# Attention kernel, one core: VectorE and TensorE streams as loops, one exponential per block, stores begun by SyncE

## Chip, cores, metric

One Trainium2 chip, one core. The metric is device time in microseconds (us) of one execution, the median of several. The kernel before takes 640.71 us (three runs, 640.48 to 640.77).

## The reference

```python
B, H, Sq, Skv, Dh = 8, 16, 16, 2048, 256          # bfloat16
def reference(q, k, v):
    scale = q.shape[-1] ** -0.5
    scores = jnp.einsum('bhqd,bhkd->bhqk', q, k) * scale
    attn = softmax(scores, axis=-1)
    return jnp.einsum('bhqk,bhkd->bhqd', attn, v)
```

There are 128 heads with 16 queries each. K and V are 134 MB each and are read once, so the work is 269 MB of loads with little arithmetic on each byte.

## The kernel before

Eight heads make a block; there are 16 blocks (`g`), each with two halves (`e`) of four heads. A half needs one K load and one V load of 4.19 MB. In each block:

- VectorE transposes K (`kt`, four pieces per half), copies the probabilities into the layout that PV needs (`px`), takes the maximum of S, and transposes P (`pt`).
- TensorE does S = QK (64 matmuls), then PV of the block before (64 matmuls).
- ScalarE does the exponential, spreads the next block's queries into QW (`qwb`), and evacuates half of the output (`evac_a`), that is, scales it and copies it out of `O_ps`.
- SyncE issues all loads. ScalarE issues the stores.

A small scheduler writes each engine's stream as a list of jobs; a job waits for the semaphores of the jobs that it depends on. The parts that matter here:

```python
def emit_exp(eng, g, h):                      # one half of S at a time
    return eng.activation(P_sb[:, 1024 * h:1024 * h + 1024],
                          S_ps[:, 2 * h:2 * h + 2, :].rearrange("p c n -> p (c n)"), ACTF.Exp,
                          bias=negm[:, g:g + 1], scale=1.0, accum_out=lsum[:, g, h:h + 1])
# ... (cut)
for g in range(G):                            # SyncE: loads only
    for u in (2 * g, 2 * g + 1):
        k_load(u)                             # waits: the transposes that read this K buffer
    if g:
        for u in (2 * g - 2, 2 * g - 1):
            v_load(u)                         # waits: PV of the block that used this V buffer
# ... (cut)
for g in range(G):                            # ScalarE
    if g >= 2:
        evac_a(g - 2)
    qwb(g + 1, 0)
    if g >= 2:
        store(g - 2)                          # two output buffers, O_fin[:, g % 2, :]
    qwb(g + 1, 1)
    softmax_act(g)                            # two exponentials
# ... (cut)
for g in range(G):                            # VectorE, all 16 blocks written out
    for e in range(2):
        for c in range(4):
            if g != 1 or e or c > 1:
                kt(g, e, c)
    if g >= 2:
        evac_b(g - 2)
    if g:
        px(g - 1, 0)
        px(g - 1, 1)
    dve_max(g)
    # ... (cut)
    for h in range(2):
        dve_pt(g, h)
    small(g)                                  # 1 / sum, times the mask
# ... (cut): TensorE: block 0 written out, blocks 1 to 14 as a hardware loop, block 15 written out
```

## Time and profile before

| | before |
|---|---|
| time | 640.71 us |
| bytes moved, mean rate from 60 to 592 us | 270.65 MB, 431 GB/s |
| TensorE / VectorE / ScalarE busy | 77% / 67% / 16% |
| VectorE's idle ahead of the transposes of K | 159.7 us in all |

From the page of the kernel before: busy time (us, share of the span, instructions), the busy tenths of the DMA engines in 40 slices, and the DMA queues (packets, MB, share of 16 engines).

```profile
span 639.2 us, 4824 instructions
...
PE 489.1 (77%) x2176; PEld 166.7 (26%) x1680; DVE 427.8 (67%) x372; ACT 99.1 (16%) x208; POOL 4.2 (1%) x7
...
DMA  9999999999999999999999999999999999999996
...
q1 hardware_dynamic: 13488, 269.51, 98.7%
q10 hardware_dynamic: 2288, 1.03, 0.6%
q8 instruction: 4, 0.07, 0.0%
q14 instruction: 6, 0.05, 0.0%
```

The DMA engines are full from the first slice to the last but one. No compute engine comes near that. q1 is SyncE's queue (loads); q10 is ScalarE's (stores); q8 and q14 fetch instructions.

The chain of waits that ended last, four pieces of it from the steady state (start us, us, what):

```profile
242.54 30.13 DMA KN<-in_k_dram
272.69 8.90 DVE KB L126 x4
281.61 30.36 DMA KN<-in_k_dram
311.99 8.90 DVE KB L126 x4
```

This reads like a latency loop: a load, four transposes that free its buffer, the next load. It isn't one, because the 30 us are mostly time in the queue behind other loads, and the DMA engines never pause. One block in the VectorE timeline (start us, us, instruction, [idle before it, and what ended that]):

```profile
282.41 8.89 DVE L126 STREAM_TRANSPOSE KB<-KN 128x2048 f32<-128x2048 f32 x4 [0.83 <-DMA KN<-in_k_dram]
291.22 0.45 DVE L313 SCALAR_TENSOR_TENSOR O_fin<-O_ps,rab,O_tmp 128x256 bf16<-128x256 f32 x1
291.58 3.44 DVE L163 COPY PT<-PC 32x1024 bf16<-32x1024 bf16 x8
295.06 2.29 DVE L148 TENSOR_REDUCE negm<-S_ps 128x1 f32<-128x2048 f32 x1
298.67 2.37 DVE L157 STREAM_TRANSPOSE PC<-P_sb 128x1024 bf16<-128x1024 bf16 x2 [1.32 <-ACT P_sb L152]
...
301.31 0.23 DVE L292 TENSOR_SCALAR rab<-mask,rinv 128x2 f32<-128x2 f32 x1
311.99 8.89 DVE L126 STREAM_TRANSPOSE KB<-KN 128x2048 f32<-128x2048 f32 x4 [10.45 <-DMA KN<-in_k_dram]
```

Two numbers are 1.32 us (wait for the exponential) and 10.45 us (wait for K, VectorE's reserve in this block: the time that it could work more before anything else became late).

### The profile page before, as it was taken

Reading aid. Unit: us, or ns where it says so; the run is one execution under the profiler, and the core shown is the slowest. Engines: PE = TensorE matmul, PEld = TensorE weight load, DVE = VectorE, ACT = ScalarE, POOL = GpSimd, SP = SyncE. Lnnn points to the kernel's source line nnn. Section 1 sums busy time; section 2 is a strip of 40 time slices with the busy share of each in tenths; the row PEclk is TensorE's granted clock in tenths of the full one; section 3 lists DMA queues with packets and bytes.
Section 4 is the critical chain, followed back from the end, with each engine's and each line's share of the span. In section 5 each row is a group of like instructions: output and inputs, shape, how many; then the busy total and the mean of one; then the engine's idle time right before and its main releaser. Section 6 shows DMA issues by size and latency. Waiting matters only on the chain.

```text
span 639.2 us, 4824 instructions
## 1 busy us (share of the span) xinstructions
PE 489.1 (77%) x2176; PEld 166.7 (26%) x1680; DVE 427.8 (67%) x372; ACT 99.1 (16%) x208; POOL 4.2 (1%) x7
## 2 busy tenths in 40 slices
PE   0857879676896768868689686787967878676998
PEld 0111313123131221312214122131311313122287
DVE  4879386693857949387492965938669395693861
ACT  2121112030120301212011120211203012030010
POOL 2000000000000000000000000000000000000000
PEclk9979979799897999899898998997979989899899
DMA  9999999999999999999999999999999999999996
GB/s 322 428 431 426 432 433 441 435 427 428 421 438 429 431 429 429 437 439 425 437 414 443 431 429 431 425 430 433 437 441 425 432 417 440 429 429 430 421 427 258
DMA packets 15786, 270.65 MB, mean 423 GB/s; under 512 B 1824, under 2 KB 4128, under 8 KB 4640
## 3 DMA queue, kind: packets, MB, share of 16 engines
q1 hardware_dynamic: 13488, 269.51, 98.7%
q10 hardware_dynamic: 2288, 1.03, 0.6%
q8 instruction: 4, 0.07, 0.0%
q14 instruction: 6, 0.05, 0.0%
HBM read 269.48 MB, written 1.05 MB: 423 GB/s over the span
## 4 chain that ended last, share of the span: by engine, by line
DMA 67%; DVE 25%; PE 7%; issue 1%; SPq 0%; DVEq 0%
DMA KN<-in_k_dram 67%; DVE KB L126 23%; PE O_ps L177 4%; PE S_ps L143 1%; PE S_ps L131 1%; DVE negm L148 0%; DVE PC L157 0%; SPq L110 0%; DVE PT L163 0%; DVE O_fin L323 0%; DVE O_fin L313 0%; DVE rab L292 0%; DVE rinv L291 0%; DVEq L410 0%; DVE ltot L289 0%
## 5 line engine op out<-in xcount | busy, mean ns | idle before, releaser
L126 DVE STREAM_TRANSPOSE KB<-KN 128x2048 f32<-128x2048 f32 x128 | 284.6, 2281 | 159.7 <-DMA KN<-in_k_dram 139.3
L143 PE MATMUL S_ps<-KB,QW 128*128 128x512 bf16 x528 | 213.1, 413 | 125.2 <-DVE KB L126 125.2
L171 PE MATMUL O_ps<-VB,PT 128*128 128x512 bf16 x896 | 200.7, 386 | 22.2 <-DMA VB<-in_v_dram 22.2
L131 PE MATMUL S_ps<-KB,QW 128*128 128x512 bf16 x496 | 203.9, 411 | 0.0
L143 PEld LDWEIGHTS S_ps<-KB,QW 128*128 128x128 bf16 x528 | 54.0, 103 | 327.7 <-issue 239.4
L171 PEld LDWEIGHTS O_ps<-VB,PT 128*128 128x128 bf16 x896 | 87.9, 99 | 138.0 <-issue 38.6
L119 ACT ACTIVATE QW<-QT 32x128 bf16<-32x128 bf16 x128 | 53.9, 421 | 320.5 <-PE S_ps L131 312.8
L163 DVE COPY PT<-PC 32x1024 bf16<-32x1024 bf16 x128 | 53.3, 416 | 4.3 <-PE O_ps L177 2.6
L157 DVE STREAM_TRANSPOSE PC<-P_sb 128x1024 bf16<-128x1024 bf16 x32 | 37.9, 1223 | 19.8 <-ACT P_sb L152 19.8
L152 ACT ACTIVATE P_sb<-S_ps,negm 128x1024 bf16<-128x1024 f32 x32 | 35.4, 1110 | 36.3 <-DVE negm L148 26.7
L148 DVE TENSOR_REDUCE negm<-S_ps 128x1 f32<-128x2048 f32 x16 | 36.7, 2292 | 4.6 <-PE S_ps L131 4.1
L308 ACT ACTIVATE O_tmp<-O_ps,rab 128x256 f32<-128x256 f32 x15 | 7.1, 474 | 157.9 <-PE O_ps L171 157.1
L177 PE MATMUL O_ps<-KN,PT 128*128 128x256 bf16 x128 | 14.4, 273 | 0.0
L177 PE MATMUL O_ps<-VB,PT 128*128 128x256 bf16 x128 | 14.1, 273 | 0.1
L177 PEld LDWEIGHTS O_ps<-VB,PT 128*128 128x128 bf16 x128 | 12.4, 98 | 2.0 <-DVE PT L163 0.6
L177 PEld LDWEIGHTS O_ps<-KN,PT 128*128 128x128 bf16 x128 | 12.4, 98 | 1.8 <-DMA KN<-in_v_dram 0.3
L323 DVE TENSOR_SCALAR O_fin<-O_ps,rab 128x256 bf16<-128x256 f32 x2 | 1.0, 483 | 11.5 <-PE O_ps L177 11.5
L313 DVE SCALAR_TENSOR_TENSOR O_fin<-O_ps,rab,O_tmp 128x256 bf16<-128x256 f32 x15 | 6.7, 448 | 1.8 <-issue 1.8
L152 ACT ACTIVATION_READ_ACCUMULATOR P_sb<-S_ps,negm 128x1 f32 x32 | 6.3, 196 | 0.0
L113 DVE STREAM_TRANSPOSE QT<-VB 128x2048 f32<-128x2048 f32 x1 | 2.3, 2311 | 5.5 <-DMA VB<-in_q_dram 5.5
L292 DVE TENSOR_SCALAR rab<-mask,rinv 128x2 f32<-128x2 f32 x16 | 3.7, 228 | 0.6
L190 POOL MEMSET PT<- 128x4096 f32 x1 | 3.5, 3512 | 0.0
(11 smaller groups left out, 7.8 us busy)
## 6 DMA issues: line engine op xcount, KB each, us to landing
KN<-in_k_dram SPq DMA_DIRECT2D x28, 4096.0 KB, 30.1
VB<-in_v_dram SPq DMA_DIRECT2D x32, 2048.0 KB, 26.5
VB<-in_v_dram SPq DMA_DIRECT2D x14, 4096.0 KB, 20.0
KN<-in_k_dram SPq DMA_DIRECT2D x8, 2048.0 KB, 15.3
KN<-in_v_dram SPq DMA_DIRECT2D x2, 2048.0 KB, 27.6
KN<-in_v_dram SPq DMA_DIRECT2D x2, 1024.0 KB, 23.1
KN<-in_v_dram SPq DMA_DIRECT2D x3, 512.0 KB, 25.8
VB<-in_q_dram SPq DMA_DIRECT2D x4, 256.0 KB, 4.4
```

The source lines that it names most:

```text
L119: ins = eng.activation(ap_of(dv, dv.offset + 32 * a + e, [[256, 4], [128, 2], [2, 16]]), ap_of(sv, sv.offset + 2 * (2 * g + e), [[64, 4], ...
L126: return eng.transpose(KBf[:, c % R_KB].rearrange("p t i -> p (t i)"), KNf[:, e].rearrange("p t i -> p (t i)")[:, n * c:n * c + n])
L131: return eng.add_instruction(mybir.InstMatmult(start_tensor_calc=start, stop_tensor_calc=stop, ldweights=False, tile_size=(128, 128), tile ...
L143: ins = mm(S_ps[:, 2 * h + c, :], QW[:, e, bp, :], rhs, start=(e == 0 and bp == 0), stop=(e == 1 and bp == 7))
L148: return eng.tensor_reduce(out=negm[:, g:g + 1], in_=S_ps[:].rearrange("p c n -> p (c n)"), axis=AX.X, op=ALU.max, negate=True)
L152: return eng.activation(P_sb[:, 1024 * h:1024 * h + 1024], S_ps[:, 2 * h:2 * h + 2, :].rearrange("p c n -> p (c n)"), ACTF.Exp, bias=negm[ ...
L157: return eng.transpose(PC[:, h].rearrange("p t x -> p (t x)"), P_sb[:, 1024 * h:1024 * h + 1024])
L163: ins = eng.tensor_copy(PT[pr, 32 * h:32 * h + 32, pr], PC[pr, h])
L171: ins = eng.matmul(O_ps[:, 0, :], PT[:, t, :], rhs, start=(t == 0), stop=(t == NT - 1))
L177: ins = eng.matmul(O_ps[:, bank, 0:D], PT[:, t, :], buf[:, t, :], start=(t == 0), stop=(t == NT - 1))
L308: j_ea[g] = J("act", "ea", lambda eng: eng.activation(O_tmp[:], src, ACTF.Copy, scale=rab[:, g, 0:1]), [("pv", g, 1) if g < last - 1 else ...
L313: j_eb[g] = J("dve", "eb", lambda eng: eng.scalar_tensor_tensor(out=O_fin[:, g % 2, :], in0=src, scalar=rab[:, g, 1:2], in1=O_tmp[:], op0= ...
```

## The change

Its intent is a shorter program with fewer operations and waits: VectorE's blocks 2 to 15 become a loop; TensorE's loop takes in block 0 and branches around PV in its first turn; each block has one exponential over 2048 columns instead of two over 1024, and so no sum of two partial sums; stores 0 to 12 go to SyncE's queue, right behind the two K loads of a later block; one output buffer serves all but the last block; and waits that follow from earlier ones are left out. The scale `rab` of a block is copied to a second place, since the loop can't index it by block.

```diff
-        def emit_exp(eng, g, h):
-            return eng.activation(P_sb[:, 1024 * h:1024 * h + 1024], ...
+        def emit_exp(eng):
+            return eng.activation(P_sb[:], S_ps[:].rearrange("p c n -> p (c n)"), ACTF.Exp,
+                                  bias=negm[:], scale=1.0, accum_out=lsum[:])
 # ... (cut) SyncE
             for u in (2 * g, 2 * g + 1):
                 k_load(u)
+            if g >= 3:
+                store("sp", g - 3)
 # ... (cut) ScalarE
             if g >= 2:
                 evac_a(g - 2)
-            qwb(g + 1, 0)
-            if g >= 2:
-                store(g - 2)
-            qwb(g + 1, 1)
+            if g == last:
+                store("act", g - 2)
             softmax_act(g)
+            qwb(g + 1)
 # ... (cut) VectorE
             if g:
+                old_rab(g - 1)
                 px(g - 1, 0)
 # ... (cut) one output buffer: block g's evacuation waits for the store of block g-1
-                op0=ALU.mult, op1=ALU.add), [("pv", g, 1), ("ea", g), ("st", g - 2) if g >= 2 else None], inc=STEP)
+                op0=ALU.mult, op1=ALU.add), [("pv", g, 1), ("ea", g), ("st", g - 1) if g else None])
 # ... (cut) the loops
+        turns = {"dve": [order["dve"][dve_head + n * x:dve_head + n * x + n] for x in range(G - 2)],
+                 "pe": [order["pe"][0:4]] + [order["pe"][6 * x - 2:6 * x + 4] for x in range(1, last)]}
+            with nc.Fori(0, STEP * len(ts), STEP, engines=engines, head_slot={eng.engine: slot}) as it:
```

More of the change, by code (lines that the diff above doesn't have):

```diff
@@ L14 @@
 R_KB = 4
+PE_SLOT, DVE_SLOT = 8, 80
 STEP = 16
@@ L58, in bass_standalone__softmax_full_bidir__sampling_kernel @@
         O_tmp = ec(nc.sbuf_tensor("O_tmp", [128, D], F32))
-        O_fin = ec(nc.sbuf_tensor("O_fin", [128, 4, D], BF16))
+        O_fin = ec(nc.sbuf_tensor("O_fin", [128, 3, D], BF16))
         ident = ec(nc.sbuf_tensor("ident", [128, 128], BF16))
         mask = ec(nc.sbuf_tensor("mask", [128, 2], F32))
-        negm = ec(nc.sbuf_tensor("negm", [128, G], F32))
-        lsum = ec(nc.sbuf_tensor("lsum", [128, G, 2], F32))
-        ltot = ec(nc.sbuf_tensor("ltot", [128, G], F32))
-        rinv = ec(nc.sbuf_tensor("rinv", [128, G], F32))
-        rab = ec(nc.sbuf_tensor("rab", [128, G, 2], F32))
+        negm = ec(nc.sbuf_tensor("negm", [128, 1], F32))
+        lsum = ec(nc.sbuf_tensor("lsum", [128, 1], F32))
+        rinv = ec(nc.sbuf_tensor("rinv", [128, 1], F32))
+        rab = ec(nc.sbuf_tensor("rab", [128, 2, 2], F32))
         S_ps = ec(nc.psum_tensor("S_ps", [128, 4, 512], F32))
@@ L72, in bass_standalone__softmax_full_bidir__sampling_kernel @@
         sem_v = [ec(nc.semaphore("s_v%d" % i)) for i in range(3)]
-        sem_st = [ec(nc.semaphore("s_st%d" % i)) for i in range(2)]
+        sem_st = ec(nc.semaphore("s_st"))
         sem_q = ec(nc.semaphore("s_q"))
@@ L76, in bass_standalone__softmax_full_bidir__sampling_kernel, with J @@
         order = {"sp": [], "pe": [], "act": [], "dve": [], "pool": []}
-        def J(eng, cls, emit, deps=(), dma=None, inc=1):
+        def J(eng, cls, emit, deps=(), dma=None):
             deps = [d for d in deps if d is not None]
@@ L85, in J @@
                 c = counters[(eng, cls)]
-                c[1] += inc
-                jb = _Job(eng, cls, emit, deps, c[0], c[1], inc)
+                c[1] += STEP
+                jb = _Job(eng, cls, emit, deps, c[0], c[1], STEP)
             order[eng].append(jb)
@@ L113, in emit_qt, with emit_qwb @@
             return eng.transpose(QT[:].bitcast(F32), QR.bitcast(F32))
-        def emit_qwb(eng, g, e):
-            for a in range(4):
-                pr = slice(32 * a, 32 * a + 32)
-                dv, sv = QW[pr, e, 0, :], QT[pr, :]
-                ins = eng.activation(ap_of(dv, dv.offset + 32 * a + e, [[256, 4], [128, 2], [2, 16]]),
-                                     ap_of(sv, sv.offset + 2 * (2 * g + e), [[64, 4], [1, 2], [D, 16]]),
-                                     ACTF.Copy, scale=scale)
+        def emit_qwb(eng, g):
+            for e in range(2):
+                for a in range(4):
+                    pr = slice(32 * a, 32 * a + 32)
+                    dv, sv = QW[pr, e, 0, :], QT[pr, :]
+                    ins = eng.activation(ap_of(dv, dv.offset + 32 * a + e, [[256, 4], [128, 2], [2, 16]]),
+                                         ap_of(sv, sv.offset + 2 * (2 * g + e), [[64, 4], [1, 2], [D, 16]]),
+                                         ACTF.Copy, scale=scale)
             return ins
@@ L145, in emit_qk, with emit_max, emit_pt, emit_px @@
             return ins
-        def emit_max(eng, g):
-            return eng.tensor_reduce(out=negm[:, g:g + 1], in_=S_ps[:].rearrange("p c n -> p (c n)"),
+        def emit_max(eng):
+            return eng.tensor_reduce(out=negm[:], in_=S_ps[:].rearrange("p c n -> p (c n)"),
                                      axis=AX.X, op=ALU.max, negate=True)
-        def emit_exp(eng, g, h):
-            return eng.activation(P_sb[:, 1024 * h:1024 * h + 1024],
-                                  S_ps[:, 2 * h:2 * h + 2, :].rearrange("p c n -> p (c n)"), ACTF.Exp,
-                                  bias=negm[:, g:g + 1], scale=1.0, accum_out=lsum[:, g, h:h + 1])
-        def emit_pt(eng, g, h):
+        def emit_exp(eng):
+            return eng.activation(P_sb[:], S_ps[:].rearrange("p c n -> p (c n)"), ACTF.Exp,
+                                  bias=negm[:], scale=1.0, accum_out=lsum[:])
+        def emit_pt(eng, h):
             return eng.transpose(PC[:, h].rearrange("p t x -> p (t x)"), P_sb[:, 1024 * h:1024 * h + 1024])
-        def emit_px(eng, g, h):
+        def emit_px(eng, h):
             for a in range(4):
@@ L183, in emit_store @@
             if e is None:
-                return eng.dma_start(dst.rearrange("e r d -> r e d"), O_fin[:, g % 2, :])
-            return eng.dma_start(dst[e, r0:r1], O_fin[2 * r0 + e:2 * r1:2, 2 + e, :])
-        j_idz = J("pool", "prep", lambda eng: eng.memset(ident[:], 0.0))
-        j_ident = J("pool", "prep", emit_ident, [j_idz])
-        j_ptz = J("pool", "prep", lambda eng: eng.memset(PT[:].bitcast(F32), 0.0))
-        j_qwz = J("dve", "prep", lambda eng: eng.memset(QW[:].bitcast(F32), 0.0))
-        j_mask = J("dve", "prep", emit_mask, [j_ident])
-        j_qz = J("dve", "prep", lambda eng: eng.memset(QR.bitcast(F32), 0.0)) if 2 * G < 32 else None
+                return eng.dma_start(dst.rearrange("e r d -> r e d"), O_fin[:, 0, :])
+            return eng.dma_start(dst[e, r0:r1], O_fin[2 * r0 + e:2 * r1:2, 1 + e, :])
+        j_idz = J("pool", "idz", lambda eng: eng.memset(ident[:], 0.0))
+        j_ident = J("pool", "ident", emit_ident, [j_idz])
+        j_ptz = J("pool", "ptz", lambda eng: eng.memset(PT[:].bitcast(F32), 0.0))
+        j_qwz = J("dve", "qwz", lambda eng: eng.memset(QW[:].bitcast(F32), 0.0))
+        j_mask = J("dve", "mask", emit_mask, [j_ident])
+        j_qz = J("dve", "qz", lambda eng: eng.memset(QR.bitcast(F32), 0.0)) if 2 * G < 32 else None
         j_q = [J("sp", "ldq", lambda eng, a=a: emit_qload(eng, a), [j_qz], dma=(sem_q, 64)) for a in range(4)]
@@ L198, in bass_standalone__softmax_full_bidir__sampling_kernel @@
         j_qwb, j_qt, j_exp, j_pt, j_px, j_max, j_rab = {}, {}, {}, {}, {}, {}, {}
-        j_ea, j_eb, j_st = {}, {}, {}
+        j_ea, j_eb, j_st, j_rold = {}, {}, {}, {}
         vparts = {NU - 2: [32, 32], NU - 4: [32, 32], NU - 1: [16, 16, 8, 8, 8, 4, 2, 2]}
@@ L231, in v_load, with store @@
                 a += n
+        def store(eng, g):
+            j_st[g] = J(eng, "st", lambda eng: emit_store(eng, g), [("eb", g)], dma=(sem_st, 16 * (g + 1)))
         for g in range(G):
@@ L241, in bass_standalone__softmax_full_bidir__sampling_kernel, with qwb @@
         v_load(NU - 1)
-        def qwb(g, e):
+        def qwb(g):
             if g < G:
-                j_qwb[g, e] = J("act", "qwb%d" % e, lambda eng: emit_qwb(eng, g, e),
-                                [("qt", 0), j_qwz, ("qk", g - 1, e, 1) if g else None], inc=STEP)
+                j_qwb[g] = J("act", "qwb", lambda eng: emit_qwb(eng, g),
+                             [("qt", 0), j_qwz, ("qk", g - 1, 1, 1) if g else None])
         def kt(g, e, c):
@@ L250, in kt @@
             before = ("qk", g, 0, h) if e else ("qk", g - 1, 1, h) if g else None
-            j_kt[g, e, c] = J("dve", "kt%d%d" % (e, h) if c % 2 else "kth", lambda eng: emit_kt(eng, e, c),
-                              [j_k[2 * g + e, h], before], inc=STEP if c % 2 else 1)
+            j_kt[g, e, c] = J("dve", "kt%d%d" % (e, c), lambda eng: emit_kt(eng, e, c), [j_k[2 * g + e, h], before])
         def qk(g, e, h):
-            j_qk[g, e, h] = J("pe", "qk", lambda eng: emit_qk(eng, e, h),
-                              [("kt", g, e, 2 * h + 1), ("qwb", g, e) if h == 0 else None,
-                               ("exp", g - 1, h) if g and e == 0 else None])
+            j_qk[g, e, h] = J("pe", "qk%d%d" % (e, h), lambda eng: emit_qk(eng, e, h),
+                              [("kt", g, e, 2 * h + 1), ("qwb", g) if e == 0 and h == 0 else None,
+                               ("exp", g - 1) if g and e == 0 else None])
         def qk_last(h):
             for c in range(2):
-                j_qk[last, 1, h] = J("pe", "qk", lambda eng, c=c, n=16: emit_qk(eng, 1, h, [c]),
-                                     [("kt", last, 1, 2 * h + c), ("qwb", last, 1)])
+                j_qk[last, 1, h] = J("pe", "qk1%d" % h if c else "qkl", lambda eng, c=c, n=16: emit_qk(eng, 1, h, [c]),
+                                     [("kt", last, 1, 2 * h + c)])
         def pv(g, h):
-            j_pv[g, h] = J("pe", "pv", lambda eng: emit_pv(eng, h),
+            j_pv[g, h] = J("pe", "pv%d" % h, lambda eng: emit_pv(eng, h),
                            [("px", g, h), ("eb", g - 1) if g and h == 0 else None]
@@ L279, in pv1 @@
                     j_pv[g, h] = j_pv[g, h, e] = J(
-                        "pe", "pv", lambda eng, t0=t0, t1=t1, n=t1 - t0: emit_pv1(eng, bank, t0, t1, v_buf(u)),
+                        "pe", "pvl", lambda eng, t0=t0, t1=t1, n=t1 - t0: emit_pv1(eng, bank, t0, t1, v_buf(u)),
                         [("px", g, h), ("eb", last - 2) if bank == 0 else None, jv])
@@ L284, in px @@
         def px(g, h):
-            j_px[g, h] = J("dve", "px%d" % h, lambda eng: emit_px(eng, g, h),
-                           [("pt", g, h), j_ptz, ("pv", g - 1, h) if g else None], inc=STEP)
+            j_px[g, h] = J("dve", "px%d" % h, lambda eng: emit_px(eng, h),
+                           [("pt", g, h), ("pv", g - 1, h) if g else j_ptz])
         def small(g):
-            js = J("dve", "sm", lambda eng: eng.tensor_reduce(
-                out=ltot[:, g:g + 1], in_=lsum[:, g, :], axis=AX.X, op=ALU.add), [("exp", g, 0), ("exp", g, 1)])
@@ L291, in small @@
-            jr = J("dve", "sm", lambda eng: eng.reciprocal(rinv[:, g:g + 1], ltot[:, g:g + 1]), [js])
-            j_rab[g] = J("dve", "sm", lambda eng: eng.tensor_scalar(
-                out=rab[:, g, :], in0=mask[:], scalar1=rinv[:, g:g + 1], scalar2=None, op0=ALU.mult), [jr, j_mask])
+            jr = J("dve", "rinv", lambda eng: eng.reciprocal(rinv[:], lsum[:]), [("exp", g)])
+            j_rab[g] = J("dve", "rab", lambda eng: eng.tensor_scalar(
+                out=rab[:, 1, :], in0=mask[:], scalar1=rinv[:], scalar2=None, op0=ALU.mult), [jr, j_rold.get(g - 1, j_mask)])
@@ L295, in softmax_act, with old_rab @@
+        def old_rab(g):
+            j_rold[g] = J("dve", "rold", lambda eng: eng.tensor_copy(rab[:, 0, :], rab[:, 1, :]),
+                          [j_rab[g], ("eb", g - 1) if g else None])
         def softmax_act(g):
-            for h in range(2):
-                j_exp[g, h] = J("act", "exp%d" % h, lambda eng, h=h: emit_exp(eng, g, h),
-                                [("max", g), ("pt", g - 1, h) if g else None], inc=STEP)
+            j_exp[g] = J("act", "exp", emit_exp, [("max", g), ("pt", g - 1, 1) if g else None])
@@ L300, in dve_max @@
         def dve_max(g):
-            j_max[g] = J("dve", "max", lambda eng: emit_max(eng, g), [("qk", g, 1, 1)])
+            j_max[g] = J("dve", "max", emit_max, [("qk", g, 1, 1)])
         def dve_pt(g, h):
-            j_pt[g, h] = J("dve", "pt", lambda eng: emit_pt(eng, g, h), [("exp", g, h)])
+            j_pt[g, h] = J("dve", "pt%d" % h, lambda eng: emit_pt(eng, h), [("exp", g)])
         def evac_a(g):
             src = O_ps[:, 0, 0:D] if g < last - 1 else O_ps[:, 1, 0:D]
-            j_ea[g] = J("act", "ea", lambda eng: eng.activation(O_tmp[:], src, ACTF.Copy, scale=rab[:, g, 0:1]),
-                        [("pv", g, 1) if g < last - 1 else ("pv", g, 1, 0), ("rab", g), ("eb", g - 1) if g else None])
+            j_ea[g] = J("act", "ea", lambda eng: eng.activation(O_tmp[:], src, ACTF.Copy, scale=rab[:, 0, 0:1]),
+                        [("pv", g, 1) if g < last - 1 else ("pv", g, 1, 0), ("rold", g), ("eb", g - 1) if g else None])
@@ L313, in evac_b @@
             j_eb[g] = J("dve", "eb", lambda eng: eng.scalar_tensor_tensor(
-                out=O_fin[:, g % 2, :], in0=src, scalar=rab[:, g, 1:2], in1=O_tmp[:],
-                op0=ALU.mult, op1=ALU.add), [("pv", g, 1), ("ea", g), ("st", g - 2) if g >= 2 else None], inc=STEP)
-        def store(g):
-            j_st[g] = J("act", "st", lambda eng: emit_store(eng, g), [("eb", g)],
-                        dma=(sem_st[g % 2], 16 * (g // 2 + 1)))
+                out=O_fin[:, 0, :], in0=src, scalar=rab[:, 0, 1:2], in1=O_tmp[:],
+                op0=ALU.mult, op1=ALU.add), [("pv", g, 1), ("ea", g), ("st", g - 1) if g else None])
         def finish(e):
-            j_eb[last, e] = J("dve", "eb", lambda eng: eng.tensor_scalar(
-                out=O_fin[:, 2 + e, :], in0=O_ps[:, (2 * last + e + 1) % 4, 0:D], scalar1=rab[:, last, e:e + 1],
+            j_eb[last, e] = J("dve", "ebl", lambda eng: eng.tensor_scalar(
+                out=O_fin[:, 1 + e, :], in0=O_ps[:, (2 * last + e + 1) % 4, 0:D], scalar1=rab[:, 1, e:e + 1],
                 scalar2=None, op0=ALU.mult), [("pv", last, 1, e), ("rab", last)])
@@ L336, in qk_block @@
                     qk(g, e, h)
-        qk_block(0)
-        for g in range(1, last):
+        for g in range(last):
             qk_block(g)
-            pv(g - 1, 0)
-            pv(g - 1, 1)
+            if g:
+                pv(g - 1, 0)
+                pv(g - 1, 1)
         qk(last, 0, 0)
@@ L349, in bass_standalone__softmax_full_bidir__sampling_kernel @@
             pv1(u, 1)
-        qwb(0, 0)
-        qwb(0, 1)
+        qwb(0)
         for g in range(G):
@@ L355, in bass_standalone__softmax_full_bidir__sampling_kernel @@
                 evac_a(g - 2)
-            qwb(g + 1, 0)
-            if g >= 2:
-                store(g - 2)
-            qwb(g + 1, 1)
+            if g == last:
+                store("act", g - 2)
             softmax_act(g)
+            qwb(g + 1)
         evac_a(last - 1)
-        store(last - 1)
+        store("act", last - 1)
         finish_store("act", 0, 0, 64)
@@ L366, in bass_standalone__softmax_full_bidir__sampling_kernel @@
         for g in range(G):
+            if g == 2:
+                dve_head = len(order["dve"])
             for e in range(2):
@@ L382, in bass_standalone__softmax_full_bidir__sampling_kernel @@
             small(g)
+        dve_tail = len(order["dve"])
         px(last, 0)
@@ L391, in bass_standalone__softmax_full_bidir__sampling_kernel @@
         tables = {"kt": j_kt, "qwb": j_qwb, "qt": j_qt, "qk": j_qk, "exp": j_exp, "pt": j_pt, "px": j_px, "max": j_max,
-                  "rab": j_rab, "ea": j_ea, "eb": j_eb, "st": j_st, "pv": j_pv}
+                  "rab": j_rab, "rold": j_rold, "ea": j_ea, "eb": j_eb, "st": j_st, "pv": j_pv}
         def resolve(d):
             return tables[d[0]][d[1] if len(d) == 2 else tuple(d[1:])] if isinstance(d, tuple) else d
-        def needs(jb):
-            need = {}
-            for d in jb.deps:
-                d = resolve(d)
-                if need.get(id(d.sem), (None, 0))[1] < d.val:
-                    need[id(d.sem)] = (d.sem, d.val)
-            return need
+        n = (dve_tail - dve_head) // (G - 2)
@@ new lines, in bass_standalone__softmax_full_bidir__sampling_kernel, with plan, one_pass, learn @@
+        turns = {"dve": [order["dve"][dve_head + n * x:dve_head + n * x + n] for x in range(G - 2)],
+                 "pe": [order["pe"][0:4]] + [order["pe"][6 * x - 2:6 * x + 4] for x in range(1, last)]}
+        n_tail = {"dve": dve_tail, "pe": 6 * last - 2}
+        def plan():
+            first = {}
+            def one_pass(fixed):
+                clock, known, prev, ptr = {}, {e: {} for e in order}, {e: {} for e in order}, {e: 0 for e in order}
+                waits, moved = {}, True
+                while moved:
+                    moved = False
+                    for e in order:
+                        while ptr[e] < len(order[e]):
+                            jb = order[e][ptr[e]]
+                            deps = [resolve(d) for d in jb.deps]
+                            if not all(id(d) in clock for d in deps):
+                                break
+                            k, w = known[e], {}
+                            def learn(c):
+                                for key, val in c.items():
+                                    if k.get(key, 0) < val:
+                                        k[key] = val
+                            for d in sorted(deps, key=lambda d: -sum(clock[id(d)].values())):
+                                if k.get(d.sem.name, 0) < d.val and (id(jb) not in fixed or d.sem.name in fixed[id(jb)]):
+                                    w[d.sem.name] = (d.sem, max(d.val, w.get(d.sem.name, (None, 0))[1]))
+                                    learn(clock[id(d)])
+                            if id(jb) in fixed:
+                                assert all(k.get(d.sem.name, 0) >= d.val for d in deps), (e, jb.cls)
+                            waits[id(jb)] = w
+                            mine = dict(k) if jb.eng == "sp" or jb.cls == "st" else {**prev[e], **k}
+                            mine[jb.sem.name] = jb.val
+                            clock[id(jb)] = mine
+                            if not (jb.eng == "sp" or jb.cls == "st"):
+                                prev[e] = {**prev[e], jb.sem.name: jb.val}
+                            ptr[e] += 1
+                            moved = True
+                assert all(ptr[e] == len(order[e]) for e in order)
+                return waits
+            w = one_pass({})
+            fixed = {}
+            for ts in turns.values():
+                for t in ts:
+                    for jb, model in zip(t, ts[-1]):
+                        fixed[id(jb)] = w[id(model)]
+            w2 = one_pass(fixed)
+            return w2, fixed
@@ L405, in emit_jobs @@
+        waits, model = plan()
         def emit_jobs(eng, jobs):
-            known = {}
             for jb in jobs:
-                for sem, val in needs(jb).values():
-                    if known.get(id(sem), 0) < val:
-                        eng.wait_ge(sem, val)
-                        known[id(sem)] = val
+                for sem, val in waits[id(jb)].values():
+                    eng.wait_ge(sem, val)
                 jb.emit(eng).then_inc(jb.sem, jb.inc)
-        def emit_stream(eng, name):
-            emit_jobs(eng, order[name])
-            for key in {"act": (last - 2, last - 1, (last, 0, 0), (last, 1, 32)), "sp": ((last, 1, 0),)}.get(name, ()):
-                eng.wait_ge(j_st[key].sem, j_st[key].val)
@@ L419, in emit_pe, with emit_loop, part @@
-        def emit_pe(eng):
-            jobs = order["pe"]
-            head, turns = jobs[:4], [jobs[4 + 6 * x:10 + 6 * x] for x in range(last - 1)]
-            emit_jobs(eng, head)
-            second = [needs(jb) for jb in turns[1]]
-            for x, turn in enumerate(turns):
-                for n0, jb in zip(second, turn):
-                    n1 = needs(jb)
-                    assert all(key in n0 and n0[key][1] + STEP * (x - 1) == val for key, (_, val) in n1.items())
-            with nc.Fori(0, STEP * len(turns), STEP, engines=OrderedEngineSet([eng.engine]), head_slot={eng.engine: 0}) as it:
-                at = {o: eng.snap(it + o) for o in sorted({val - STEP for n0 in second for _, val in n0.values()})}
-                for jb, n0 in zip(turns[0], second):
-                    for sem, val in n0.values():
-                        eng.wait_ge(sem, at[val - STEP])
-                    jb.emit(eng).then_inc(jb.sem, jb.inc)
-            emit_jobs(eng, jobs[4 + 6 * len(turns):])
+        def emit_loop(eng, name, slot):
+            ts = turns[name]
+            first, full = ts[0], ts[-1]
+            lag = STEP * (len(ts) - 1)
+            for x, turn in enumerate(ts):
+                assert len(turn) == len(full if x else first)
+                for jb in turn:
+                    for key, (_, val) in waits[id(jb)].items():
+                        assert model[id(jb)][key][1] + STEP * (x + 1 - len(ts)) == val, (x, jb.cls, key)
+            engines = OrderedEngineSet([eng.engine])
+            def part(jobs):
+                for jb in jobs:
+                    for sem, val in model[id(jb)].values():
+                        eng.wait_ge(sem, at[val - lag])
+                    jb.emit(eng).then_inc(jb.sem, jb.inc)
+            with nc.Fori(0, STEP * len(ts), STEP, engines=engines, head_slot={eng.engine: slot}) as it:
+                at = {o: eng.snap(it + o) for o in sorted({val - lag for jb in full for _, val in model[id(jb)].values()})}
+                part(full[:len(first)])
+                if len(first) < len(full):
+                    nc.br_lt(it, STEP, on_true="after", on_false="rest", engines=engines)
+                    with nc.body("rest", valid_engines=engines):
+                        part(full[len(first):])
+                        nc.br("after", engines=engines)
+                    nc.switch_bb("after")
@@ L438, in bass_standalone__softmax_full_bidir__sampling_kernel, with emit_stream @@
+        def emit_stream(eng, name, slot=None):
+            a = 0
+            if name in turns:
+                a = order[name].index(turns[name][0][0])
+                emit_jobs(eng, order[name][:a])
+                emit_loop(eng, name, slot)
+                a = n_tail[name]
+            emit_jobs(eng, order[name][a:])
+            for key in {"act": (last - 1, (last, 0, 0), (last, 1, 32)), "sp": ((last, 1, 0),)}.get(name, ()):
+                eng.wait_ge(j_st[key].sem, j_st[key].val)
         emit_stream(nc.sync, "sp")
@@ L439, in bass_standalone__softmax_full_bidir__sampling_kernel @@
         emit_stream(nc.scalar, "act")
-        emit_stream(nc.vector, "dve")
+        emit_stream(nc.vector, "dve", DVE_SLOT)
         emit_stream(nc.gpsimd, "pool")
-        emit_pe(nc.tensor)
+        emit_stream(nc.tensor, "pe", PE_SLOT)
 _INS = ['q', 'k', 'v']
```

## The prediction

> **What bounds it now.** The DMA: 270.65 MB (DMA view), with a share of about 1.0 in three-microsecond windows from 3 to 633 us. VectorE is 67% busy, TensorE 77%, ScalarE 16%. In steady state the chain of waits repeats every 39.03 us: a K load 30.13 us from issue to landing, four transposes 8.90 us, the next K load. It looks like a latency loop, but that time is queueing: a block's four loads of 4.19 MB in 39.05 us are 430 GB/s, what the slices show. A microsecond more on VectorE is one less of queueing, while the queue holds work.
>
> Reserve, from the timeline: V loads are issued at 311.41 with one K load (9.8 us at 430 GB/s) still queued; K loads at 281.61 with V loads (about 20 us) queued; VectorE waits 10 us per block for K. So about 9 us in each block.
>
> **What changes.**
> - One exponential of 2048 columns replaces two of 1110 ns plus reads of 196 ns. From 474 ns at 256 columns and 1110 ns at 1024 I estimate 1.96 us, 0.45 us less ScalarE time per block. The transpose of P waits for the whole: VectorE's wait goes from 1.32 to about 2.3 us, into its idle time.
> - Q weights for the next block (8 activations of 0.42 us) follow the exponential: ready 3.5 us after it, before the transposes of K that the next QK needs; only block 1 slips, about 1.4 us, with V loads queued.
> - VectorE loses a reduce (0.11 us), gains a copy of the scale (estimate 0.1 to 0.2 us).
> - Stores join SyncE's queue behind two K loads, before V loads that wait longer anyway (for PV). The Trainium skill ("DMA: Bandwidth & Descriptors", Issuing engines are not separate DMA queues) says that DMAs share the same 16 engines whoever starts them; in this trace the stores' queue takes 0.6% of the engines' time. Moving it changes tenths of a per cent at most. The single output buffer makes an evacuation wait for the store before it, which lands with the K load ahead of it, about 9 us early.
> - Loops on VectorE, a branch over PV on TensorE: once per block, where these engines wait. The skill ("Runtime: NRT & Kernel Launch", Instruction fetch mechanics) warns that a taken branch outside the fetched pages stalls on a DMA fetch; in this trace TensorE's loop shows none beyond its wait for K, and instruction queues move 0.12 MB. I expect branches under 1 us.
> - Fewer waits: below what the trace resolves.
>
> **On the critical path.** Steady state: nothing, DMA bytes are equal. Head: DMA bound, nothing. Tail: the chain ends with four copies (to 608.19) and 256 matmuls back to back, 28.35 us; the copy of the scale comes before: +0.1 to +0.4 us. Stores: under 1 us either way. Sum: 640.71 + 0.3 = about 641.0 us.
>
> Predicted: 641.0 us, range 638.5 to 643.5. Chance of over 2% faster 0.01, within 2% 0.96, over 2% slower 0.03.
>
> **What would show it.** Period of the chain 39.0 to 39.2 us; DMA share unchanged; one queue with all 270.5 MB; ScalarE busy down from 99 to about 90 us; VectorE's wait for P up from 19.8 to about 35 us, its wait for K down by as much; the last matmul run starting 0.1 to 0.4 us later.
>
> **What would make it wrong.** A fetch at the loop's branch queued behind 8 MB of loads (10 to 20 us a turn): 5 to 20% slower. Stores' 512-byte packets stalling the load ring over 0.3 us a block: up to 1% slower. A store landing too late for the evacuation delays PV, V loads, then everything. A throttled clock in the tail: 1 to 3 us.

## The result

The changed kernel takes 641.08 us (six runs, 640.9 to 641.12) beside 640.68 us (640.43 to 640.77) for the kernel before in the same rounds. The ratio is 1.0007, with a 95% interval of 0.9994 to 1.0019: the same. It is correct.

The same lines of the changed kernel's page:

```profile
span 639.6 us, 4902 instructions
...
PE 489.3 (76%) x2176; PEld 166.6 (26%) x1680; DVE 428.3 (67%) x371; ACT 93.7 (15%) x176; POOL 4.2 (1%) x7
...
DMA  9999999999999999999999999999999999999996
...
q1 hardware_dynamic: 15360, 270.36, 99.2%
q10 hardware_dynamic: 416, 0.18, 0.1%
```

The stores have moved from q10 to q1, and nothing else in these lines has moved by more than a few us. From 60 to 592 us both kernels draw 431 GB/s. The same block of VectorE:

```profile
283.29 8.89 DVE L127 STREAM_TRANSPOSE KB<-KN 128x2048 f32<-128x2048 f32 x4 [1.41 <-PE S_ps L132]
292.10 0.45 DVE L318 SCALAR_TENSOR_TENSOR O_fin<-O_ps,rab,O_tmp 128x256 bf16<-128x256 f32 x1
292.64 0.17 DVE L299 COPY rab<-rab 128x2 f32<-128x2 f32 x1
292.74 3.46 DVE L163 COPY PT<-PC 32x1024 bf16<-32x1024 bf16 x8
296.23 2.29 DVE L149 TENSOR_REDUCE negm<-S_ps 128x1 f32<-128x2048 f32 x1
300.78 2.37 DVE L157 STREAM_TRANSPOSE PC<-P_sb 128x1024 bf16<-128x1024 bf16 x2 [2.26 <-ACT P_sb L153]
...
303.29 0.23 DVE L295 TENSOR_SCALAR rab<-mask,rinv 128x2 f32<-128x2 f32 x1
312.08 8.89 DVE L127 STREAM_TRANSPOSE KB<-KN 128x2048 f32<-128x2048 f32 x4 [8.56 <-DMA KN<-in_k_dram]
```

The wait for the exponential grew by 0.94 us (1.32 to 2.26), the copy and its wait put 0.28 us between the evacuation's start and the copies of P (0.36 us from start to start before, 0.64 us after), and the wait for K shrank from 10.45 to 8.56 us. K itself arrives at the same time: the transposes start at 311.99 us before and 312.08 us after, and at 351.06 and 351.19 us in the next block. So the period is unchanged at 39.1 us, and the change was paid out of VectorE's idle time.

Two things in the trace were not foreseen. The transpose of Q, VectorE's third instruction, starts at 8.66 us instead of 7.60 us. And the changed kernel's last 16 matmuls wait for the last piece of V, where the kernel before ran its last 128 without a wait in this profile. The last group of the changed kernel's TensorE timeline, then the last one of the kernel before:

```profile
635.00 1.92 PE L177 MATMUL O_ps<-KN,PT 128*128 128x256 bf16 x16 [0.19 <-DMA KN<-in_v_dram]
...
622.22 14.36 PE L177 MATMUL O_ps<-KN,PT 128*128 128x256 bf16 x128
```

The changed kernel's chain that ended last accordingly goes back to that load, not, as I had it, to VectorE's copies before the last run of matmuls. That is no mark of the change alone: in the second profile of the kernel before (e1), too, the chain goes back to a V load, for which its last 96 matmuls wait:

```profile
625.73 10.79 PE L177 MATMUL O_ps<-KN,PT 128*128 128x256 bf16 x96 [1.00 <-DMA KN<-in_v_dram]
```

### The profile page after: what moved, and what is told of

Its sections match the earlier page's. It is cut to its first block, busy times and chain, and to the rows that moved or that the text cites. A ratio compares the mean times of both kernels' runs of the same rounds, so it can differ in the third digit from the quotient of the medians.

```text
span 639.6 us, 4902 instructions
## 1 busy us (share of the span) xinstructions
PE 489.3 (76%) x2176; PEld 166.6 (26%) x1680; DVE 428.3 (67%) x371; ACT 93.7 (15%) x176; POOL 4.2 (1%) x7
## 5 line engine op out<-in xcount | busy, mean ns | idle before, releaser
L127 DVE STREAM_TRANSPOSE KB<-KN 128x2048 f32<-128x2048 f32 x128 | 284.8, 2281 | 142.8 <-DMA KN<-in_k_dram 124.1
L144 PE MATMUL S_ps<-KB,QW 128*128 128x512 bf16 x528 | 213.2, 413 | 124.1 <-DVE KB L127 116.1
L153 ACT ACTIVATE P_sb<-S_ps,negm 128x2048 bf16<-128x2048 f32 x16 | 31.5, 1967 | 399.2 <-DVE negm L149 399.2
L157 DVE STREAM_TRANSPOSE PC<-P_sb 128x1024 bf16<-128x1024 bf16 x32 | 37.9, 1222 | 33.8 <-ACT P_sb L153 33.8
L177 PEld LDWEIGHTS O_ps<-KN,PT 128*128 128x128 bf16 x128 | 12.3, 98 | 2.6 <-DMA KN<-in_v_dram 1.1
L324 DVE TENSOR_SCALAR O_fin<-O_ps,rab 128x256 bf16<-128x256 f32 x2 | 1.0, 484 | 12.3 <-PE O_ps L177 7.4
L299 DVE COPY rab<-rab 128x2 f32<-128x2 f32 x15 | 2.5, 167 | 1.2
```

The source lines that it names most:

```text
L127: return eng.transpose(KBf[:, c % R_KB].rearrange("p t i -> p (t i)"), KNf[:, e].rearrange("p t i -> p (t i)")[:, n * c:n * c + n])
L144: ins = mm(S_ps[:, 2 * h + c, :], QW[:, e, bp, :], rhs, start=(e == 0 and bp == 0), stop=(e == 1 and bp == 7))
L153: return eng.activation(P_sb[:], S_ps[:].rearrange("p c n -> p (c n)"), ACTF.Exp, bias=negm[:], scale=1.0, accum_out=lsum[:])
L157: return eng.transpose(PC[:, h].rearrange("p t x -> p (t x)"), P_sb[:, 1024 * h:1024 * h + 1024])
L177: ins = eng.matmul(O_ps[:, bank, 0:D], PT[:, t, :], buf[:, t, :], start=(t == 0), stop=(t == NT - 1))
```

## The experiments

Two questions are worth chip time. First, is "paid out of the reserve" the true reason for the null result, and what is each part of the change worth when the reserve is gone? Second, what are the 0.4 us? The theories: A, the activation table load, now earlier, disturbs the Q loads; B, chance; C, stores inside the ring of the loads (SyncE's queue) cost DMA time; D, my prediction, the copy of the scale delays the last matmuls; E, an early instruction fetch delays Q.

In this table "minus before" is the difference of the mean times to the runs of the kernel before in the same rounds.

| run | median us (runs) | minus before |
|---|---|---|
| e1, kernel before again | 640.51 (5) | -0.06 |
| e2, changed kernel again | 641.13 (5) | +0.50 |
| e3, changed, stores by ScalarE | 640.61 (5) | 0.00 |
| e4, changed, table load late | 641.17 (5) | +0.48 |
| e9, before, stores by SyncE | 640.90 (5) | +0.41 |
| e10, e3 repeated | 640.78 (5) | +0.26 |
| e11, changed, TensorE's block 0 out of the loop | 640.91 (5) | +0.44 |
| e5, before + four reductions (8.8 us) on VectorE per block | 649.50 (4) | +8.5 |
| e6, changed + the same | 674.95 (4) | +34.3 |
| e12, e6 with VectorE's loop unrolled | 661.83 (4) | +21.4 |
| e7, before, a quarter of the loads' bytes | 513.29 (4) | |
| e8, changed, a quarter of the loads' bytes | 517.10 (4) | |

### e1 and e2: both kernels again

No edit.

> The kernel before against itself: ratio 1.000, and so the noise of the pairing (under 0.0003). All theories expect Q to land and its transpose to start at 7.6 us, give or take what chance does; theory B (chance moves the first landings) expects a scatter of about 1 us here, theory A (the earlier table load of ScalarE) expects 7.6 again within 0.2 us.

> The changed kernel again: about 641.1 us, 0.4 us over the kernel before (ratio 1.0006). Theory A (table load at 0.73 us instead of 2.01 us disturbs the Q loads): the transpose of Q starts again at about 8.7 us. Theory B (chance): it starts anywhere between 7.6 and 8.7 us. Theory D (my prediction, the copy of the scale delays the last matmuls): the last run of matmuls starts later than 608.24 us; the first profile already speaks against it (about 607.9 us).

Measured: 640.51 us (ratio 0.9999, 0.9985 to 1.0012) and 641.13 us (1.0007, 0.9993 to 1.0021). Q's transpose starts at 7.60 us again in e1 and at 9.45 us in e2. So the pairing adds no difference of its own, the 0.4 to 0.5 us repeat, and a late Q belongs to the changed kernel; B falls as the account of Q. D falls too: the last run of 256 matmuls began at 608.24 us and 607.09 us in two profiles of the kernel before, and at 607.87 and 607.58 us in two of the changed kernel. The start moves by 1.1 us from run to run of the same program, and the changed kernel's lies inside that.

### e3 and e10: stores back on ScalarE

```diff
-            if g >= 3:
-                store("sp", g - 3)
 # ScalarE
-            if g == last:
+            if g >= 2:
                 store("act", g - 2)
```

> The changed kernel, but every full store is begun by ScalarE on its own queue, as before. Theory C (stores inside the ring of the loads cost time): back to 640.7 us, 0.4 us below the changed kernel. Theories A and B: as the changed kernel, within 0.15 us of 641.1 us. The stores land in about 10 us instead of 29.6 us; nothing waits for either.

> Repeat of the changed kernel with stores begun by ScalarE, on another draw of chip and rounds. Theory C: 640.6 us, equal to the kernel before within 0.2 us. If the first run of it was luck: about 641.1 us.

Measured: 640.61 us (ratio 0.9998, 0.9985 to 1.0012), and in the repeat 640.78 us (1.0004, 0.9990 to 1.0018). Landing takes 10.5 us in the repeat instead of 29.6 us. The first run agrees with C; the repeat lies between, 0.06 us above what C allowed. Q's transpose started at 9.76 us in e3, the latest of all runs, and e3 was the fastest variant of the changed kernel (640.87 us in the profiled execution itself): no cost of a late Q shows.

### e4: the table load made late

```diff
             for jb in jobs:
+                if jb is order["act"][0]:
+                    eng.wait_ge(j_qwz.sem, j_qwz.val)     # VectorE's memset of QW
```

> The changed kernel, but ScalarE's first job waits for VectorE's memset of QW as before, which puts the activation table load back to about 2.0 us. Theory A: the transpose of Q starts at about 7.6 us again and the time falls by 0.3 to 1 us, to 640.1 to 640.8 us. Theories B and C: no change, 641.1 us.

Measured: 641.17 us (ratio 1.0007), Q's transpose at 9.22 us. The edit didn't do what was intended: the table load came at 11.61 us, after Q's transpose had begun, and not at 2.0 us.

```profile
11.61 1.28 ACT L120 ACT_TABLE_LOAD   x1 [11.61 <-DVE QT L113]
```

So it can't have disturbed the loads of Q in this run, and Q was late all the same. A falls.

### e9: only the stores moved, on the kernel before

```diff
 # SyncE
                 k_load(u)
+            if g >= 3:
+                store("sp", g - 3)
 # ScalarE
-            if g >= 2:
-                store(g - 2)
+            if g == last:
+                store("act", g - 2)
```

> The kernel before with only one part of the change: stores 0 to 12 begun by SyncE behind the K loads, as in the changed kernel. Theory C (stores inside the ring of the loads cost about 0.04 us each): 641.1 us, 0.4 to 0.6 us over the kernel before. If the 0.5 us between the changed kernel and its variant with stores on ScalarE was chance, or belongs to the single output buffer: 640.7 us.

Measured: 640.90 us, 640.88 to 641.13, beside 640.38 to 640.87 for the kernel before: +0.41 us, with the rest of the change absent. Taken together, the five sets with stores in the loads' ring (the first result, e2, e4, e9, e11) lie 0.41 to 0.50 us over the kernel before, and the three with stores on ScalarE (e1, e3, e10) lie -0.06 to +0.26 us. That supports C. It doesn't settle it: the 95% interval of each ratio is about 0.8 us wide to either side, and e10 leaves some 0.2 us open. The traces don't settle it either. By their packet records the last load packet ends at 635.50 and 635.46 us in the two profiles of the kernel before, at 635.84 and 635.86 us in the two of the changed kernel, and at 635.68 us in e9, so most of the difference is there when the loads end. But with stores on ScalarE it ends at 635.73 and 635.69 us (e3 and e10), no earlier than in e4 and e11 with stores on SyncE (635.69 and 635.66 us).

### e11: TensorE's block 0 out of the loop

```diff
-                 "pe": [order["pe"][0:4]] + [order["pe"][6 * x - 2:6 * x + 4] for x in range(1, last)]}
+                 "pe": [order["pe"][6 * x - 2:6 * x + 4] for x in range(1, last)]}
```

> The changed kernel with TensorE's block 0 taken out of the loop again, as before. Theory E (the jump to TensorE's loop head at once makes an early 16 KB instruction fetch, seen between 0 and 6 us in the traces of the changed kernel and between 30 and 45 us in those of the kernel before, and it holds up one DMA engine's part of the Q loads): no instruction fetch in the first 6 us and the transpose of Q starts at 7.6 to 7.8 us. If the fetch is not the cause, it still starts at 8.7 to 9.8 us. The time stays at 641.1 us in both, since the variant with stores on ScalarE had Q latest of all (9.76 us) and was no slower.

Measured: Q's transpose at 7.71 us, and 640.91 us. The DMA queues of the first 6 us of e2 and the first 12 us of e11 (kind: packets, MB, share of 16 engines in that window):

```profile
q1 hardware_dynamic: 172, 1.02, 73.1%
q8 instruction: 1, 0.02, 1.4%
q14 instruction: 1, 0.00, 0.0%
```

```profile
q1 hardware_dynamic: 353, 3.42, 87.2%
```

With the loop entered at once, one instruction packet of 0.02 MB (q8) travels among the Q loads; its share, 1.4% of 16 engines in 6 us, is 1.3 us of one engine. Q was 1.85 us late in that run; why it is more than the packet's own time stays open. With block 0 written out, no instruction packet is seen before 30 us, and Q is on time. In the kernel before, too, the packet comes between 30 and 45 us. E is confirmed, and no cost of the late Q (1.1 to 2.2 us over 7.60) shows in the time: e11 lies 0.44 us over the kernel before with Q on time, e2 and e4 0.50 and 0.48 us with Q late. The Trainium skill ("Runtime: NRT & Kernel Launch", Instruction fetch mechanics) says that a taken branch outside the fetched pages forces a DMA fetch; this trace agrees, and adds that here the loads queued beside the fetch were hurt, not the engine that branched.

### e5 and e6: use up the reserve

Each block gets four extra reductions of S on VectorE, with unused results.

```diff
         def emit_max(eng):
+            for i in range(4):
+                eng.tensor_reduce(out=junk[:, i:i + 1], in_=S_ps[:].rearrange("p c n -> p (c n)"),
+                                  axis=AX.X, op=ALU.max, negate=True)
```

> The kernel before with four extra reductions of S (4 x 2.29 us = 9.2 us of VectorE per block, results unused). Its VectorE waits 10.0 to 10.4 us for K per block, so if the DMA bounds it and VectorE has that reserve, the steady state keeps its period of 39.1 us; only the end grows, by 9 us at most, since the last block's chain has no loads to hide behind: 641 to 650 us. If instead the loop of K load and transposes were latency-bound, every block would grow by 9 us: about 780 us.

> The changed kernel with the same 9.2 us of extra VectorE work per block. Its VectorE waits only 7.7 to 8.6 us for K, 1.5 to 2.4 us less than before. If the cost of the change was paid out of that reserve, this work no longer fits: 0.6 to 1.5 us too much in each of 14 blocks, 9 to 21 us more than the kernel before with the same extra work. If the change cost the engines nothing, the two are equal within 1 us.

Measured: 649.50 us (ratio 1.0132, 1.0115 to 1.0149) and 674.95 us (1.0538, 1.0520 to 1.0555). In e5, from the first extra reduction of a block to the reduction that was there before:

```profile
297.66 8.88 DVE L150 TENSOR_REDUCE junk<-S_ps 128x1 f32<-128x2048 f32 x4
306.46 2.28 DVE L152 TENSOR_REDUCE negm<-S_ps 128x1 f32<-128x2048 f32 x1
```

Each block's extra work took 8.8 us (297.66 to 306.46 us), a little under the 9.2 us of the sum, and 16 blocks of it are 141 us; the kernel before absorbs all but 8.5 us of it, and its last load packet ends only 2.2 us later (637.71 us by the packet records). That shows that it was the DMA, not the loop of load and transposes, that set its time. The changed kernel no longer absorbs it: 25.4 us apart, more than the 9 to 21 us expected. (The mean granted TensorE clock was 0.886 in e6 and 0.910 in e5, but TensorE was busy 488.7 and 488.6 us, so the clock doesn't make the difference.) From the first extra reduction of one block to that of the next, the mean of twelve blocks is 38.63 us in e5 (109.00 to 572.60) and 39.82 us in e6 (119.25 to 597.09): 1.19 us each, 14 us in twelve. Most of what was not expected is in the first turn of VectorE's loop, 46.54 us (72.71 to 119.25) beside 38.48 us (70.52 to 109.00). The VectorE timeline of e6 there, and one turn later:

```profile
88.56 0.23 DVE L299 TENSOR_SCALAR rab<-mask,rinv 128x2 f32<-128x2 f32 x1
95.20 8.89 DVE L128 STREAM_TRANSPOSE KB<-KN 128x2048 f32<-128x2048 f32 x4 [6.41 <-issue]
...
135.09 0.23 DVE L299 TENSOR_SCALAR rab<-mask,rinv 128x2 f32<-128x2 f32 x1
135.64 8.89 DVE L128 STREAM_TRANSPOSE KB<-KN 128x2048 f32<-128x2048 f32 x4 [0.32 <-issue]
```

The entry into the loop costs 6.41 us, every later turn 0.30 to 0.32 us. In the stretch from 88 to 100 us two instruction packets are seen on q14, 0.02 MB in all:

```profile
q1 hardware_dynamic: 186, 4.64, 90.5%
q14 instruction: 2, 0.02, 0.3%
```

### e12: the same without VectorE's loop

```diff
-            if name in turns:
+            if name in turns and name != "dve":
                 a = order[name].index(turns[name][0][0])
```

> The changed kernel with 9.2 us of extra VectorE work per block, its VectorE loop unrolled (same waits otherwise). Its looped form took 674.95 us, the kernel before with the same work 649.5 us. If the loop's branch (0.30 us between the last small operation and the next transposes) and the one entry fetch cost what the traces show, 4 us for the branches, and up to 8 us for the first turn, go: 662 to 671 us. If the loop costs nothing: 675 us. What remains over 649.5 us belongs to the single exponential (0.94 us a block), the copy of the scale with its wait (0.28 us), and the head.

Measured: 661.83 us (ratio 1.0330, 1.0314 to 1.0345), 13.1 us less than e6 and just below the 662 to 671 us expected. The same place in e12, and one turn later:

```profile
88.25 0.23 DVE L299 TENSOR_SCALAR rab<-mask,rinv 128x2 f32<-128x2 f32 x1
88.79 8.89 DVE L128 STREAM_TRANSPOSE KB<-KN 128x2048 f32<-128x2048 f32 x4 [0.31 <-issue]
...
127.96 0.23 DVE L299 TENSOR_SCALAR rab<-mask,rinv 128x2 f32<-128x2 f32 x1
128.09 2.31 DVE L128 STREAM_TRANSPOSE KB<-KN 128x2048 f32<-128x2048 f32 x1
```

The first turn falls from 46.54 to 39.73 us (72.38 to 112.11), 6.8 us, and the other twelve from 39.82 to 39.32 us on average (112.11 to 583.93), 6.0 us: 12.8 of the 13.1 us. So VectorE's loop is 6.8 us once plus about 0.5 us a turn, when nothing hides it. (A packet on q14 is seen at 92.81 us here, too, without a stall, so a packet alone costs nothing.) The remaining 12.3 us to the kernel before with the same work are the other parts: 0.69 us a block in these twelve blocks, and the start. No run takes these parts (the single exponential, the copy of the scale, the one output buffer) one by one.

### e7 and e8: a quarter of the bytes

All K loads after block 1 and all V loads after block 0 fetch a quarter of their rows. Their outputs are wrong, which doesn't matter for the times. All work of the engines stays.

```diff
-    KN[:, e], ku[u]
+    KN[:, e, 0:16], ku[u, :, 0:16]
 # V: the first quarter of each part, from block 1 on
-    v_buf(u)[:, a:a + n, :], vu[u, :, a:a + n, :]
+    v_buf(u)[:, a:a + m, :], vu[u, :, a:a + m, :]       # m = n if g == 0 else max(1, n // 4)
```

> The kernel before with a quarter of the bytes in each K and V load after the first ones (wrong result on purpose; all instructions of the engines kept). The DMA no longer bounds it: the period becomes what the engines' chain needs, 39.1 - 10.2 = about 29 us, in all 450 to 490 us.

> The changed kernel with the same quarter of the bytes. If its engines' chain is 1.5 to 2.4 us longer per block, as its shorter wait for K says, it is 22 to 36 us (5 to 8%) slower than the kernel before with a quarter of the bytes. If the change cost the engines nothing, equal within 2 us. About 0.9 us per block should be the wait for the one exponential (2.26 instead of 1.32 us); the rest must show as the branch, or as waits of QK.

Measured: 513.29 us and 517.10 us. Both expectations were wrong: 450 to 490 us for the first, and 22 to 36 us of difference where there are 3.8. The first missed although the period was nearly right (29.97 us for about 29): the beginning and the end were underrated, since block 2 begins at 70.25 us and the last run of 256 matmuls takes 28 us. For the second, the VectorE timelines of e7, then of e8, tell why:

```profile
309.45 8.88 DVE L126 STREAM_TRANSPOSE KB<-KN 128x2048 f32<-128x2048 f32 x4
320.38 8.89 DVE L126 STREAM_TRANSPOSE KB<-KN 128x2048 f32<-128x2048 f32 x4 [2.05 <-PE S_ps L131]
...
339.42 8.88 DVE L126 STREAM_TRANSPOSE KB<-KN 128x2048 f32<-128x2048 f32 x4
```

```profile
314.64 8.89 DVE L127 STREAM_TRANSPOSE KB<-KN 128x2048 f32<-128x2048 f32 x4 [0.30 <-issue]
324.08 8.89 DVE L127 STREAM_TRANSPOSE KB<-KN 128x2048 f32<-128x2048 f32 x4 [0.55 <-issue]
...
344.60 8.89 DVE L127 STREAM_TRANSPOSE KB<-KN 128x2048 f32<-128x2048 f32 x4 [0.30 <-issue]
```

Both have the same period, 29.97 us (309.45 to 339.42) and 29.96 us (314.64 to 344.60). Without the DMA's limit the next one is a loop through TensorE and VectorE. TensorE, with 64 QK and 64 PV matmuls a block, about 0.216 us each (13.81 us for a block's 64 PV matmuls in the chain of e7), is busy 28.02 of the 29.97 us and waits the rest, 1.21 and 0.74 us, for transposes of K; VectorE waits 2.05 us per block for QK to free the buffers of K. The changed kernel pays its extra VectorE time out of that wait, which falls to a gap of 0.55 us: 1.5 us a block, itemised from these timelines as 0.94 us (exponential), 0.26 us (copy of the scale and its wait) and 0.26 us (the branch, about 0.39 us, less a reduction saved). The 3.8 us arise once, at the start. When block 1's scale is computed, e8 is already 3.78 us behind (72.18 and 68.40 us), 1.56 us of it since Q's transpose. The transposes of block 2 then start at 75.57 us instead of 70.25, after an idle of 3.16 us at the loop's entry, with two packets on q14 between 73 and 76 us, where e7 waits 1.62 us for K. Thereafter the distance doesn't grow (the last evacuation is at 513.36 and 509.37 us).

## Why the prediction was right

1. *The bound.* The DMA bounds the kernel, and the 30 us of the chain are queueing. Shown by e5: 141 us of added VectorE work cost 8.5 us. The reserve, "about 9 us in each block", was right: 8.8 us a block fitted, nearly all of it.
2. *The exponential.* I estimated 1.96 us; it took 1.967 us. VectorE's wait for P went from 1.32 to 2.26 us (2.3 foretold), in all from 19.8 to 33.8 us (35 foretold), and its wait for K fell from 139.3 to 124.1 us. ScalarE's busy time fell to 93.7 us, not about 90: 0.34 us a block instead of 0.45.
3. *Stores.* "Under 1 us either way" holds: +0.41 us alone (e9), as far as timing resolves it. They land in 29.6 us (the median); by that, one issued at 292.58 us is down by about 322 us, and the next evacuation comes at 332.12 us, 10 us later. The Trainium skill ("DMA: Bandwidth & Descriptors", Issuing engines are not separate DMA queues) holds for the rate, 431 GB/s either way.
4. *The branches.* "I expect branches under 1 us" was right for every turn but the first. The entry into VectorE's loop fetches instructions and stalls 3.2 us (e8) to 6.4 us (e6). I had judged from TensorE's loop in the kernel before, where no stall showed beyond its wait for K. In the changed kernel VectorE's entry falls into a wait of 6.20 us that K ends, so it costs nothing. And the entry of TensorE's loop delays Q by 1.1 to 2.2 us, also without a cost that shows.
5. *The step that failed, with the right total.* I laid the +0.3 us on the end: "the copy of the scale comes before: +0.1 to +0.4 us". The runs don't show it. The last run of matmuls starts within the scatter of the kernel before, and it has slack, since it ends by waiting for the last piece of V. What the runs show in its place is that the loads themselves end 0.34 to 0.40 us later. The stores' term, for which I had put zero into the sum, is by the times the likelier source (+0.41 us with the stores alone moved, e9), though the traces of e3 and e10 don't bear it out. So the total was right by luck in this term, and which part of 0.4 us belongs to what stays open at the level of 0.2 us. Late landing of a store with one output buffer, the other risk that I named, was not tried.

## What to carry to other kernels

When the DMA engines are full, ask of each change only whether the queue can run dry: how long each engine waits for data per block is the budget, and a change that costs less than it reads as no change. That doesn't make it free: here 1.5 us a block and one fetch of several microseconds at a loop's entry were spent from about 10 us of reserve, and once other work used up the reserve, the two "equal" kernels were 25 us apart. Measure such a change by adding known work until the reserve is gone; taking the bound away instead may only uncover slack in the next limit, as the quarter loads did with the loop through TensorE and VectorE.

## What the Trainium skill lacked or had wrong

- "Runtime: NRT & Kernel Launch", Instruction fetch mechanics: no duration for the fetch after a taken branch. Here: 3.16 us on VectorE with the loads cut to a quarter, 6.41 us among full loads, once per loop; later turns left a gap of 0.30 to 0.32 us, and only three instruction packets travelled in e6 from 130 to 620 us, in twelve turns, so not every turn fetches. Nor does that section say that a fetch can delay loads: with one packet among the loads at the start, Q landed 1.1 to 2.2 us late.
- "Advanced Engine Details and Errata", Control Flow Timing: a compare-and-branch at about 108 ns. That alone isn't what a turn costs: 0.30 us of idle from the last operation to the first of the next turn (with a register operation and the waits).
- "DMA: Bandwidth & Descriptors", Issuing engines are not separate DMA queues: right about the rate; that section is silent on latency (how rings take turns stands elsewhere on the page, without a figure for this case). The same 64 KB stores land in 10.6 us from their own queue and in 29.6 us behind two queued loads.
- "DMA: Bandwidth & Descriptors", Where 436 GB/s comes from: the statement that the HBM side (about 358 GB/s) binds for loads from HBM doesn't hold for this one core: 431 GB/s from 60 to 592 us, near the page's fabric ceiling of 435. The page's own 16 MB measurement (425) agrees with the runs, and its note there gives about 358 for two cores streaming at once; the sentence lacks that condition.
